# A sliding-window attention and SwiGLU kernel: a staged prologue, and q, k and x transposed by DMA instead of on TensorE

## The chip, the cores and the metric

The kernel runs on one core of one Trainium2 chip. The metric is the device time of one execution in microseconds (us). The profile's span runs from the first to the last instruction and is about 1.7 us shorter than the time. Most figures inside an execution below are on the span's clock.

The text uses the profile's names: PE is TensorE, PEld its weight loads, DVE VectorE, ACT ScalarE, POOL GpSimd, SP SyncE; SPq is the time in which SP issues a DMA. L327 is line 327 of that kernel's file, and the same function can have another line number in another kernel.

## The reference

```python
# q, k, v: [8 batches, 8 heads, 576 positions, 64], float32
scores = (1 / 8) * q @ k.transpose(0, 1, 3, 2)
mask = (rel >= 0) & (rel < 64)                 # rel = query position - key position
attn = softmax(where(mask, scores, -1e9)) @ v
x = attn.transpose(0, 2, 1, 3).reshape(4608, 512)
g = x @ w_gate                                 # 512 x 1536
out = (g * sigmoid(g) * (x @ w_val)) @ w_out   # 1536 x 512, result float32
```

## The kernel before

The 4608 tokens are cut in 36 chunks of 128 (n) for the attention and in 9 groups of 512 (c) for the gate, value and output products. For a chunk, `T` transposes k and q, `Sx` makes the scores of four heads, `AV` multiplies with v and divides by the row sum into `xb`, and `X` transposes `xb` into `xT`. `F(c, f)` makes one 128-wide slice of gate and value for 512 tokens, `O(c, u)` the output of 128 tokens. All of it is bf16 with float32 sums. A helper records the operations in program order, and each engine executes its own in that order, waiting on semaphores. In the main loop, chunk n = 4c+u+4 runs ahead of the group that needs it:

```python
def T(self, n):                      # on TensorE: 8 transposes into one bank, 3 evacuations
    def pe(e):
        for w, src in ((0, kn), (1, qn)):
            for c in range(4):
                r = e.transpose(tb[:, w, c, :], src[:, 2 * c:2 * c + 2, :], ident[:, :])
        return r
    ...  # DVE copies k into kT, ACT and DVE one half each of q into qz (its other half is zero)

for c in range(1, NFC):
    for u in range(4):
        n = 4 * c + u + 4
        load(n + 4)
        self.F(c, 3 * u);     self.AV(n, 0); self.Sx(n + 1, 0)
        self.F(c, 3 * u + 1); self.AV(n, 1); self.Sx(n + 1, 1)
        self.O(c - 1, u);     self.X(n)       # cut: conditions for the ends, and c == 1
        self.F(c, 3 * u + 2); self.T(n + 2)   # k and q two chunks ahead
```

The softmax here doesn't subtract the row's maximum and nothing guards it: scores larger than these inputs give would overflow.

Of the kernel before, what the change touches and what calls it, by code (L numbers as in the profile page):

```python
# [149 lines left out]
class _Kernel:  # L150
    NQ = 4
    NV = 8
# [13 lines left out]
    def alloc(self):  # L166
# [9 lines left out]
        self.mask = sb("mask", 4 * 64)  # L176
        self.Wg = sb("Wg", NK * DFF)[:, :].rearrange("p (c f) -> p c f", c=NK)
# [3 lines left out]
        self.qn = [hd(t) for t in ring("qn", self.NQ, DM)]  # L181
        self.kn = [hd(t) for t in ring("kn", self.NQ, DM)]
# [3 lines left out]
        self.qza = sb("qz", self.NZ * 4 * 2 * 128)[:, :].rearrange("p (r c e t) -> p r c e t", r=self.NZ, c=4, e=2)  # L186
        self.qz = [self.qza[:, r] for r in range(self.NZ)]
        self.fq, self.fk = [t[:, :].rearrange("p (h j d) -> p h j d", h=H, j=4) for t in ring("f", 2, H * 256, F32)]
        self.cq, self.ck = [t[:, :].rearrange("p (j h d) -> p j h d", j=4, h=H) for t in ring("c", 2, H * 256)]
        self.nmask = sb("nmask", 4 * 64)  # L190
# [4 lines left out]
        self.xT = [t[:, :].rearrange("p (c t) -> p c t", c=NK) for t in ring("xT", self.NX, NK * 512)]  # L195
        self.sig = ring("sig", self.NS, 512)
        self.uu = ring("uu", self.NS, 512)
        self.hT = [t[:, :].rearrange("p (f t) -> p f t", f=NF) for t in ring("hT", self.NH, NF * 512)]
# [22 lines left out]

    def init(self):
        g = self.g
        ident, mask = self.ident, self.mask
        g.op("dve", lambda e: e.memset(self.wz[:, :], 0.0), writes=["wz"])
        g.op("dve", lambda e: e.memset(ident[:, :], 0.0), writes=["ident"])  # L226
        g.op("dve", lambda e: e.memset(self.nmask[:, :], 0.0), writes=["nmask"])
        g.op("dve", lambda e: e.memset(mask[:, :], 1.0), writes=["mask"])
        g.op("dve", lambda e: e.memset(self.wup[:, :], 0.0), writes=["wup"])
        g.op("act", lambda e: e.activation(self.wup[:, :], self.wup[:, :], ACTF.Exp), writes=["wup"])  # L230
        zz = self.qza
        g.op("dve", lambda e: e.memset(zz[64:128, :, :, 0, :], 0.0), writes=[("qz", i, p, 0) for i in range(self.NZ) for p in range(4)])
        g.op("dve", lambda e: e.memset(zz[0:64, :, :, 1, :], 0.0), writes=[("qz", i, p, 1) for i in range(self.NZ) for p in range(4)])
        g.op("dve", lambda e: e.memset(self.kT[:, :, 0:64], 0.0), writes=[("kT", -1, p) for p in range(4)])
        g.op("dve", lambda e: e.memset(self.vb[0][0:64, :, 0:66], 0.0), writes=[("vb", 0, 0)])
        self.init_va(0)

    def init_pt(self):
        g = self.g
        for i in range(self.NP):  # L240
            p = self.pt[i]
            g.op("dve", lambda e, p=p: e.memset(p[:, :, 64:128], 0.0), writes=[("pt", i, 0), ("pt", i, 1)])

    def init_va(self, i0):
        g = self.g
        for i in range(i0, i0 + 4):
            va = self.va[i]
            g.op("dve", lambda e, va=va: e.memset(va[:, :, 64:80], 1.0), writes=[("va", i)])

    def init_pool_a(self):  # L250
        ident = self.ident
        self.g.op("pool", lambda e: e.affine_select(
            out=ident[:, :], in_=ident[:, :], compare_op=ALU.not_equal, fill=1.0, base=0,
            pattern=[[-1, 128]], channel_multiplier=1), writes=["ident"])
# [11 lines left out]
    def load_qk(self, n):  # L266
        i = n % self.NQ
        for dst, src, nm in ((self.qn[i], self.q, "qn"), (self.kn[i], self.k, "kn")):
            parts = list(self.segs(128 * n, 128))
            for j, (r, b, s, L) in enumerate(parts):  # L270
                d = dst[r:r + L]
                a = src[b, :, s:s + L, :].rearrange("h p d -> p h d")
                ks = [(nm, i, j)] if len(parts) > 1 else [(nm, i, 0), (nm, i, 1)]
                self.g.op("pool", lambda e, d=d, a=a: e.dma_start(d, a), writes=ks, dma=True)  # L274

    def first_loads(self):
        for half in range(2):
            hs = slice(4 * half, 4 * half + 4)
            for eng, dst, src, nm in (("sp", self.fk, self.k, "fk"), ("act", self.fq, self.q, "fq")):
                d = dst[:, hs].rearrange("p h j d -> p h (j d)")  # L280
                a = src[0, hs, 0:512, :].rearrange("h (p j) d -> p h (j d)", j=4)
                self.g.op(eng, lambda e, d=d, a=a: e.dma_start(d, a), writes=[(nm, half)], dma=True)

    def first_cast(self, which, half):
        hs = slice(4 * half, 4 * half + 4)
        dst, src, eng = (self.ck, self.fk, "dve") if which == "k" else (self.cq, self.fq, "act")
        d = dst[:, :, hs].rearrange("p j h d -> p h j d")
        rk, wk = [("f" + which, half)], [("c" + which, half)]
        if eng == "dve":
            self.g.op("dve", lambda e: e.tensor_copy(d, src[:, hs]), reads=rk, writes=wk)  # L290
        else:
            self.g.op("act", lambda e: e.activation(d, src[:, hs], ACTF.Copy), reads=rk, writes=wk)

    def first_T(self, which, half):
        g = self.g
        bank, bk = self.bank("a")
        tb = bank[:, :].bitcast(BF).rearrange("p (c j t) -> p c j t", c=2, j=4)
        src = self.ck if which == "k" else self.cq

        def pe(e):  # L300
            for c in range(2):
                pr = 2 * half + c
                for j in range(4):
                    r = e.transpose(tb[:, c, j, :], src[:, j, 2 * pr:2 * pr + 2, :], self.ident[:, :])
            return r

        g.op("pe", pe, reads=["ident", ("c" + which, half)], writes=[bk])
        prs = slice(2 * half, 2 * half + 2)
        if which == "k":
            kd = self.kT[:, prs, 64:576].rearrange("p c (t j) -> p c t j", j=4)  # L310
            ks = tb.rearrange("p c j t -> p c t j")
            kk = [("kT", n, p) for n in range(4) for p in (2 * half, 2 * half + 1)]
            g.op("dve", lambda e: e.tensor_copy(kd, ks), reads=[bk], writes=kk)
            return
        for e_, eng in ((0, "act"), (1, "dve")):
            ps = slice(64 * e_, 64 * e_ + 64)
            zk = [("qz", n, p, e_) for n in range(4) for p in (2 * half, 2 * half + 1)]

            def ev(e, ps=ps, e_=e_, eng=eng):
                for c in range(2):  # L320
                    d = self.qza[ps, :, 2 * half + c, e_, :].rearrange("p r (t j) -> p r t j", j=4)
                    a = tb[ps, c].rearrange("p j (r t) -> p r t j", r=4)
                    r = e.activation(d, a, ACTF.Copy) if eng == "act" else e.tensor_copy(d, a)
                return r

            g.op(eng, ev, reads=[bk], writes=zk)

    def warm(self, count):
        bank, bk = self.ps[7], ("ps", 7)

        def pe(e):
            for _ in range(count):
                r = e.matmul(bank[:, :], self.wz[:, 0:128], self.wz[:, :], start=True, stop=True)
            return r

        self.g.op("pe", pe, reads=["wz"], writes=[bk])

    def load_v(self, n):
        g = self.g
        i = n % self.NV  # L340
        va = self.va[i]
        parts = list(self.segs(128 * n, 128))
        for j, (r, b, s, L) in enumerate(parts):
            d = va[r:r + L, :, 0:64]
            a = self.v[b, :, s:s + L, :].rearrange("h p d -> p h d")
            ks = [("va", i, j)] if len(parts) > 1 else [("va", i, 0), ("va", i, 1)]
            g.op("pool", lambda e, d=d, a=a: e.dma_start(d, a), writes=ks, dma=True)  # L347
        vb = self.vb[i]
        lo = [("va", i, 0), ("va", i)]
        hi = [("va", i, 0 if len(parts) == 1 else 1), ("va", i)]  # L350
# [16 lines left out]

    def T(self, n):
        g = self.g
        iq, iz = n % self.NQ, n % self.NZ  # L370
        qn, kn, qz = self.qn[iq], self.kn[iq], self.qz[iz]
        bank, bk = self.bank("a")
        tb = bank[:, :].bitcast(BF).rearrange("p (w c t) -> p w c t", w=2, c=4)
        ident = self.ident

        def pe(e):
            for w, src in ((0, kn), (1, qn)):
                for c in range(4):
                    r = e.transpose(tb[:, w, c, :], src[:, 2 * c:2 * c + 2, :], ident[:, :])  # L379
# [339 lines left out]
```

## Time and profile before

The median time is 373.5 us (2 runs, 373.46 to 373.55). The span is best cut in three. The marks are the starts, in the trace, of ScalarE's first tanh of group c=2 and of group c=8 (each follows the first gate product of its group by about 1 us):

| part | before, us | what is in it |
|---|---|---|
| early, to c=2 | 99.0 | loads of weights, attention of chunks 0 to 11, c=0, c=1 |
| steady, c=2 to c=7 | 229.5 | 24 periods, median 9.64 |
| tail, c=8 | 43.3 | no attention left |

The chain that ended last in the kernel before, between 182 and 193 us: start, duration, what.

```profile
182.18 0.22 PE ps L460 x4
182.41 1.73 PE ps L485 x8
184.13 0.45 PE ps L379 x8
184.58 1.73 PE ps L485 x8
186.31 0.03 PE ps L438
...
186.55 0.28 PE ps L408 x4
186.83 1.73 PE ps L485 x8
...
188.84 0.40 PE ps L408 x4
189.24 0.05 issue
189.29 2.54 PE ps L508 x11
```

One period is all PE: three gate/value groups (L485), one output group (L508), the k/q transposes (L379, 0.45 us), the x transposes (L460, 0.22 us), scores (L408) and AV (L438 and L439). Time is saved there by taking work off TensorE, or by making its pieces shorter.

### The profile page before, as it was taken

Reading aid. Unit: us, or ns where it says so; the run is one execution under the profiler, and the core shown is the slowest. Engines: PE = TensorE matmul, PEld = TensorE weight load, DVE = VectorE, ACT = ScalarE, POOL = GpSimd, SP = SyncE. Lnnn points to the kernel's source line nnn. Section 1 sums busy time; section 2 is a strip of 40 time slices with the busy share of each in tenths; the row PEclk is TensorE's granted clock in tenths of the full one; section 3 lists DMA queues with packets and bytes.
Section 4 is the critical chain, followed back from the end, with each engine's and each line's share of the span. In section 5 each row is a group of like instructions: output and inputs, shape, how many; then the busy total and the mean of one; then the engine's idle time right before and its main releaser. Section 6 shows DMA issues by size and latency. Waiting matters only on the chain.

```text
span 371.8 us, 6649 instructions
## 1 busy us (share of the span) xinstructions
PE 353.7 (95%) x2604; PEld 193.6 (52%) x2649; DVE 254.5 (68%) x550; ACT 151.9 (41%) x260; POOL 108.6 (29%) x139
## 2 busy tenths in 40 slices
PE   6779989999899999999999999999999999999997
PEld 2644555555455555555555555555555555444444
DVE  5758876688867777777777777777777777645530
ACT  2743625445444344343344444434434444233321
POOL 8995435343222222322222222422220000000000
PEclk9899999999999999999999999999999999999999
DMA  8999999979947777788878877788881000001002
GB/s 237 201 203 175 206 171 216 173 53 86 86 69 86 88 84 87 82 89 88 91 81 92 86 83 79 74 85 90 88 90 37 30 29 30 28 30 56 28 30 113
DMA packets 126302, 35.61 MB, mean 96 GB/s; under 512 B 108288, under 2 KB 121792, under 8 KB 126272
## 3 DMA queue, kind: packets, MB, share of 16 engines
q0 software_dynamic: 113152, 17.83, 64.8%
q1 hardware_dynamic: 11920, 16.18, 13.5%
q10 hardware_dynamic: 1200, 1.18, 1.0%
q8 instruction: 21, 0.34, 0.4%
q14 instruction: 9, 0.07, 0.1%
HBM read 37.75 MB, written 9.44 MB: 127 GB/s over the span
## 4 chain that ended last, share of the span: by engine, by line
PE 79%; DVE 12%; DMA 4%; ACT 2%; issue 2%; SPq 1%; POOLq 0%
PE ps L485 41%; PE ps L508 24%; PE ps L408 5%; DVE uu L493 4%; DVE hT L495 3%; PE ps L379 3%; DMA va<-in_v_dram 2%; PE ps L460 2%; PE ps L438 2%; PE ps L439 2%; DVE xb L448 2%; DMA vb<-va 2%; ACT sig L491 1%; DVE pt L426 1%; ACT qz L385 1%
## 5 line engine op out<-in xcount | busy, mean ns | idle before, releaser
L493 DVE SCALAR_TENSOR_TENSOR uu<-sig,ps 128x512 bf16<-128x512 bf16 x108 | 74.1, 686 | 62.5 <-ACT sig L491 62.4
L485 PE MATMUL ps<-xT,Wv 128*128 128x512 bf16 x430 | 110.8, 379 | 0.1
L485 PE MATMUL ps<-xT,Wg 128*128 128x512 bf16 x408 | 105.7, 379 | 3.8 <-DVE xT L467 1.7
L508 PE MATMUL ps<-Wo,hT 128*128 128x512 bf16 x401 | 93.2, 379 | 2.0 <-DVE rc L445 1.0
L491 ACT ACTIVATE sig<-ps 128x512 bf16<-128x512 f32 x108 | 64.0, 592 | 44.3 <-PE ps L485 44.3
L274 POOL DMA_DIRECT2D qn<-in_q_dram x36 | 30.6, 853 | 163.0 <-PE ps L379 160.7
L495 DVE SCALAR_TENSOR_TENSOR hT<-uu,ps 128x512 bf16<-128x512 bf16 x108 | 74.2, 687 | 3.7
L485 PEld LDWEIGHTS ps<-xT,Wv 128*128 128x128 bf16 x432 | 42.3, 98 | 51.0
L508 PEld LDWEIGHTS ps<-Wo,hT 128*128 128x128 bf16 x420 | 39.8, 98 | 43.9 <-DVE hT L495 1.0
L420 ACT ACTIVATE pt<-ps 128x512 bf16<-128x512 f32 x72 | 42.8, 597 | 33.5 <-PE ps L408 30.9
L485 PEld LDWEIGHTS ps<-xT,Wg 128*128 128x128 bf16 x432 | 38.3, 98 | 32.6 <-DVE xT L467 2.0
L513 ACT ACTIVATE ost<-ps 128x512 f32<-128x512 f32 x35 | 20.9, 597 | 70.5 <-PE ps L508 70.5
L385 ACT ACTIVATE qz<-ps 64x512 bf16<-64x512 bf16 x32 | 18.9, 591 | 57.8 <-DVE kT L384 57.8
L347 POOL DMA_DIRECT2D va<-in_v_dram x40 | 34.7, 876 | 1.3 <-DVE ident L226 0.8
L408 PE MATMUL ps<-qz,kT 128*128 128x128 bf16 x288 | 30.4, 224 | 2.0 <-ACT qz L385 0.4
L448 DVE TENSOR_TENSOR xb<-ps,rc 128x256 bf16<-128x256 f32 x72 | 30.6, 425 | 2.5
L274 POOL DMA_DIRECT2D kn<-in_k_dram x36 | 30.7, 859 | 0.8 <-DMA Wv<-in_moe_w_val_dram 0.8
L467 DVE COPY xT<-ps 128x512 bf16<-128x512 bf16 x32 | 13.6, 424 | 24.0 <-PE ps L460 24.0
L438 PE MATMUL ps<-vb,pt 128*128 128x65 bf16 x288 | 26.9, 193 | 1.0 <-issue 0.4
L426 DVE TENSOR_TENSOR pt<-pt,mask 128x512 bf16<-128x512 bf16 x64 | 26.6, 416 | 1.5 <-ACT pt L420 1.4
L438 PEld LDWEIGHTS ps<-vb,pt 128*128 128x128 bf16 x288 | 22.5, 98 | 8.7 <-issue 1.1
L439 PE MATMUL ps<-va,pt 128*128 128x65 bf16 x288 | 27.0, 193 | 0.0
(54 smaller groups left out, 208.2 us busy)
## 6 DMA issues: line engine op xcount, KB each, us to landing
out_dram<-ost SPq DMA_DIRECT2D x35, 256.0 KB, 2.0
vb<-va SPq DMA_DIRECT2D x71, 80.0 KB, 2.1
va<-in_v_dram POOLq DMA_DIRECT2D x32, 128.0 KB, 4.5
qn<-in_q_dram POOLq DMA_DIRECT2D x28, 128.0 KB, 3.5
kn<-in_k_dram POOLq DMA_DIRECT2D x28, 128.0 KB, 4.4
Wo<-in_moe_w_out_dram POOLq DMA_DIRECT2D x2, 768.0 KB, 17.8
Wg<-in_moe_w_gate_dram POOLq DMA_DIRECT2D x5, 256.0 KB, 10.9
Wv<-in_moe_w_val_dram POOLq DMA_DIRECT2D x5, 256.0 KB, 11.5
```

The costliest lines, as they stand in the source:

```text
L274: self.g.op("pool", lambda e, d=d, a=a: e.dma_start(d, a), writes=ks, dma=True)
L347: g.op("pool", lambda e, d=d, a=a: e.dma_start(d, a), writes=ks, dma=True)
L408: r = e.matmul(sv[:, w, c], self.kT[:, pr, k0:k0 + 128], qz[:, pr, :, 64 * w:64 * w + 64], start=not bias, stop=True)
L420: g.op("act", lambda e: e.activation(po, si, ACTF.Exp, scale=SCALE), reads=[bk], writes=[pk])
L438: e.matmul(av[:, j, :], pt[:, h, 0:128], vb[:, h, 0:65], start=True, stop=False)
L439: r = e.matmul(av[:, j, :], pt[:, h, 64:192], va[:, h, 0:65], start=False, stop=True)
L448: g.op("dve", lambda e: e.tensor_tensor(xo, av[:, :, 0:64], rb, ALU.mult), reads=[bk, ("rc", ir)], writes=[("xb", ix, half)])
L485: r = e.matmul(bank[:, :], W[:, kk, f * 128:f * 128 + 128], xT[:, kk, :], start=(kk == 0), stop=(kk == NK - 1))
L491: g.op("act", lambda e: e.activation(sig[:, :], G[:, :], ACTF.Tanh, scale=0.5), reads=[gk], writes=[("sig", i)])
L493: g.op("dve", lambda e: e.scalar_tensor_tensor(uu[:, :], sig[:, :], 1.0, G[:, :], ALU.add, ALU.mult), reads=[("sig", i), gk], writes=[("uu ...
L495: g.op("dve", lambda e: e.scalar_tensor_tensor(hT[:, f, :], uu[:, :], 0.5, V[:, :], ALU.mult, ALU.mult), reads=[("uu", i), vk], writes=[(" ...
L508: r = e.matmul(OB[:, :], hT[:, f, 128 * u:128 * u + 128], self.Wo[:, f, :], start=(f == 0), stop=(f == NF - 1))
```

## The change

Its intent is to take every transpose off TensorE from chunk 4 on, and to start the products sooner.

1. Chunks 0 to 3 run in two stages of 256 tokens, with scores on PE tiles of 64 rows, and the first two gate/value groups are cut in halves around the second stage.
2. From chunk 4 on, k, q and x are transposed by DMAs on the sync queue. q is loaded into a buffer with zeros between the heads, so that its transpose has the zero halves that the scores need: 128x1024 instead of 128x512.
3. The later weights are loaded between chunks 4 to 7, and the padding of q is zeroed before that, by VectorE.
4. The order of c=0 and c=1 is new, with half-width groups in c=1.

```diff
     def T(self, n):
-        (8 PE transposes and 3 evacuations)
+        g.op("sp", lambda e: e.dma_start_transpose(kd, kn), reads=[("kn", iq, j) for j in range(2)],
+             writes=[("kT", n)], dma=True)
+        g.op("sp", lambda e: e.dma_start_transpose(qd, qn), reads=[("qn", iq, j) for j in range(4)],
+             writes=[("qz", iz)], dma=True)
+    def X(self, n):
+        self.g.op("sp", lambda e: e.dma_start_transpose(xo, xb), reads=[("xb", ix, 0), ("xb", ix, 1)],
+                  writes=[("xT", it, u)], dma=True)
     def A(self, n):
             self.AV(n, 0)
             self.AV(n, 1)
+            self.X(n)
+    def prep(self, n):
+            self.T(n)
+            self.shift_v(n)
... (prologue, loads, c=0 and c=1 cut)
-        for c in range(1, NFC):
+        for c in range(2, NFC):
             for u in range(4):
                 n = 4 * c + u + 4
-                load(n + 4)
+                self.load(n + 3)
                 self.F(c, 3 * u)
-                    (AV(n, 0), Sx(n + 1, 0))
+                self.A(n)
+                self.prep(n + 1)
                 self.F(c, 3 * u + 1)
-                    (AV(n, 1), Sx(n + 1, 1))
+                if n + 1 < NCH:
+                    self.Sx(n + 1, 0)
                 self.O(c - 1, u)
-                    (X(n))
+                if n + 1 < NCH:
+                    self.Sx(n + 1, 1)
                 self.F(c, 3 * u + 2)
-                    (T(n + 2))
```

## The prediction

> **What bounds it now.** TensorE. The page gives PE 95% of the 371.8 us span, and the chain of waits is 79% PE, 12% DVE. In steady state (chain from 170 to 220 us) one 128-token period is 9.63 us, all PE: three gate/value groups of 1.73, one output group 2.59, the q/k transposes 0.45, the x transposes 0.22, AV 0.50, scores 0.68 with small gaps. Before that, the first gate/value matmul starts at 24.8 us, held by the v loads and v shifts (the chain shows 9.0 and 5.6 us of DMA), and from 34 to 51 us the chain runs on VectorE.
>
> **What the change removes.** For 32 chunks the q/k and x transposes: 32 x 0.67 = 21 us of PE time, all critical in steady state. VectorE loses 1.27 us per chunk (0.42 + 0.43 + 0.42) and ScalarE 0.59. This should largely remove the VectorE-bound stretch at 34 to 51 us. The staged prologue should start the gate/value matmuls some 6 us sooner. With nothing new in the way, I estimate 343 to 353 us.
>
> **What it adds, and where it lands.** On the sync queue, per chunk: transposes of x(n), k(n+1), q(n+1), beside two v shifts and an output store. The order is the problem. That queue issues in program order, and x(n) comes first: it waits for xb(n), the last VectorE work of AV(n). So k(n+1) and q(n+1) can't be issued earlier, though their inputs have long been loaded. On PE, scores of n+1 follow AV(n) after one gate/value group only, 1.73 us.
>
> Timed from the end of the group before AV(n): scores could start at 0.50 + 1.73 = 2.23 us. xb(n) is done at about 2.65 us: final uu and hT 0.7 each, two reciprocal and multiply pairs of 0.6. Then three issues and a landing. Ordinary copies on this queue take 0.34 to 0.60 us to issue and land 2.0 to 2.1 us after issue; no transposing DMA is in this trace. The Trainium skill ("VectorE: DVE Perf Modes", The three transpose paths) gives 1309 ns for one 128x128 through the DMA crossbar, against 390 on TensorE; here q alone is eight such blocks, half of them zero padding. I estimate 0.5 + 0.5 us for the issues ahead of q and 2.8 us for q: scores start at 6.4 us, a PE stall near 4.2 us in each of 23 periods. The period becomes about 13 us instead of 8.96, and VectorE and DMA have slack in it.
>
> **Sum.** c=0 and c=1: no VectorE stretch and an earlier start, but stalls at the scores of chunks 8, 11 and 12 and at the xT halves, so c=2 starts at about 95 us (before: 96). Then 24 x 13.1 = 314, and the tail without attention 44: about 450 us. Even with 2.3 us of stall per chunk it is near 400.
>
> **Prediction:** 450 us, 80% range 398 to 520. Faster by over 2%: 0.06; within 2%: 0.04; slower by over 2%: 0.90.
>
> **What would show it.** Right: PE waits of 3 to 6 us before the score matmuls, released by the DMA into kT or qz, once per chunk from c=2 to c=7; the sync queue waiting for xb; PE busy below 85%; a period of 12 to 15 us up to the last attention chunk, then 7.8 us. The first gate/value matmul before 20 us. Wrong: the scores not waiting, and a period near 9 us.
>
> **What would make it wrong.** Transposes that land in well under 2 us, which would leave about 390. Long issue times (over 1 us each), DMA contention with the loads (4.2 us to landing now) or a lower granted clock after the stalls would bring 500 or more. Late weights, now split by chunk loads, could add to the first 100 us.

## More of the kernel before

The page of the kernel before: the span; then PE's busy time; then, in 40 equal slices of the span, PE's busy tenths and the clock granted to TensorE in tenths.

```profile
span 371.8 us, 6649 instructions
...
PE 353.7 (95%) x2604; PEld 193.6 (52%) x2649; DVE 254.5 (68%) x550; ACT 151.9 (41%) x260; POOL 108.6 (29%) x139
...
PE   6779989999899999999999999999999999999997
...
PEclk9899999999999999999999999999999999999999
```

## The result, and the profile after

The changed kernel takes 595.3 us (2 runs, 594.8 to 595.8) against 373.5: the ratio is 1.594, with a 95% interval of 1.589 to 1.598. Ratios in this text are the mean time of one kernel's fast runs over that of the other's of the same rounds, so they are not quite the ratio of the medians quoted. The result is correct. The forecast of slower was right; its 450 us, and its range up to 520, were not.

| part | before | forecast | after |
|---|---|---|---|
| early, to c=2 | 99.0 | about 98 (95, where it counts 96 for the kernel before; 99.0 on this mark) | 151.0 |
| steady, 24 periods | 229.5 | 314 | 399.8 |
| tail | 43.3 | 44 | 43.3 |
| median period | 9.64 | 13.1 | 17.06 |

The same lines of the page, for the changed kernel:

```profile
span 594.1 us, 6153 instructions
...
PE 399.7 (67%) x2337; PEld 193.8 (33%) x2337; DVE 222.6 (37%) x472; ACT 132.4 (22%) x232; POOL 129.6 (22%) x173
...
PE   6676367744666777666667766666677666669998
...
PEclk9598787878788877778888777788877777888999
```

PE has fewer instructions and more busy time, and its clock stays at seven or eight tenths in the mean of a slice until the attention is over (inside a period it is half or full, see below). One period of the chain of the changed kernel shows both reasons:

```profile
355.42 0.70 DVE uu L521
...
356.14 0.69 DVE hT L524
...
357.51 0.42 DVE xb L387
357.93 0.61 DVE uu L521
358.54 0.62 SPq L394
359.16 0.04 issue
359.20 1.26 SPq L327
...
360.56 3.06 DMA qz<-qn
...
363.67 0.61 PE ps L351 x4
364.28 4.70 PE ps L561 x12
368.98 0.22 PE ps L351 x4
369.20 2.60 PE ps L503 x12
```

VectorE ends xb of chunk n at 357.93. Then SyncE issues x (L394; its instruction starts at 357.96 and takes 1.20 us), then k of chunk n+1 (L327, 1.26 us), then q, which lands 3.06 us after its issue begins. Only then can the scores (L351) start. TensorE has had nothing for 5.84 us. And the output group that follows (L561, 12 matmuls) takes 4.70 us instead of 2.59: its weight loads are 0.43 us apart, twice the 0.216 that a matmul of 512 columns takes elsewhere. The clock records of the trace give 0.50 from 361.60 to 368.43 (6.83 us) and 1.00 for the 10.24 us before and after; TensorE has work for 4.76 of those 6.83 us. All 23 periods of the steady part that hold attention show the same two lengths, in sum 17.07 us, and the median period is 17.06.

The waits of the changed kernel's engines, then of its sync queue (engine, line, what it waited for: us in total, times, longest), three and one of many:

```profile
PE ps L351 <- DMA qz<-qn: 156.3, 29, 7.6
POOL qn L287 <- DVE qn L234: 22.5, 1, 22.5
PE ps L503 <- DMA xT<-xb: 16.8, 2, 9.4
```

```profile
SPq L394 <- DVE uu L521: 141.7, 25, 9.7
```

The first line is the wait described above. The last is x at the head of the sync queue, waiting for VectorE (the profile names the VectorE instruction that runs beside the end of xb) while k and q, long loaded, stand behind it. The two others belong to the early part: the load of q of chunk 4 stands 22.5 us in the GpSimd queue behind the zeroing of its padding, with the weights and loads of later chunks behind it; and twice the products of c=1 wait for x.

The DMA issues of the changed kernel (what, queue, count, KB each for plain copies, median us from the start of the issue to landing):

```profile
out_dram<-ost SPq DMA_DIRECT2D x35, 256.0 KB, 2.0
...
kT<-kn SPq DMA_TRANSPOSE x32, 2.5
...
qz<-qn SPq DMA_TRANSPOSE x32, 3.1
xT<-xb SPq DMA_TRANSPOSE x32, 2.3
```

### The profile page after: what moved, and what is told of

Read it like the earlier page. It is cut to its first block, busy times and chain, and to the rows that moved or that the text cites. A ratio compares the mean times of both kernels' runs of the same rounds, so it can differ in the third digit from the quotient of the medians.

```text
span 594.1 us, 6153 instructions
## 1 busy us (share of the span) xinstructions
PE 399.7 (67%) x2337; PEld 193.8 (33%) x2337; DVE 222.6 (37%) x472; ACT 132.4 (22%) x232; POOL 129.6 (22%) x173
## 4 chain that ended last, share of the span: by engine, by line
PE 48%; DMA 20%; DVE 15%; SPq 10%; ACT 3%; issue 2%; POOL 1%; POOLq 0%
PE ps L561 23%; PE ps L503 19%; DMA qz<-qn 16%; SPq L327 6%; DVE uu L521 6%; DVE xb L387 5%; PE ps L351 4%; DVE hT L524 4%; SPq L394 3%; ACT sig L513 3%; DMA va<-in_v_dram 2%; DVE rc L381 1%; DMA Wg<-in_moe_w_gate_dram 1%; DMA vb<-va 1%; POOL qn L287 1%
## 5 line engine op out<-in xcount | busy, mean ns | idle before, releaser
L561 PE MATMUL ps<-Wo,hT 128*128 128x512 bf16 x420 | 144.2, 517 | 0.0
L351 PE MATMUL ps<-qz,kT 128*128 128x128 bf16 x256 | 30.4, 262 | 157.1 <-DMA qz<-qn 156.3
L503 PE MATMUL ps<-xT,Wg 128*128 128x512 bf16 (+1 forms) x464 | 119.0, 382 | 24.0 <-DMA xT<-xb 16.8
L503 PE MATMUL ps<-xT,Wv 128*128 128x512 bf16 (+1 forms) x464 | 117.9, 379 | 0.0
L521 DVE SCALAR_TENSOR_TENSOR uu<-sig,ps 128x512 bf16<-128x512 bf16 (+1 forms) x114 | 74.9, 657 | 70.8 <-ACT sig L513 70.6
L513 ACT ACTIVATE sig<-ps 128x512 bf16<-128x512 f32 (+1 forms) x114 | 65.6, 575 | 124.9 <-PE ps L503 124.9
L561 PEld LDWEIGHTS ps<-Wo,hT 128*128 128x128 bf16 x420 | 54.0, 131 | 79.5 <-issue 62.9
L351 PEld LDWEIGHTS ps<-qz,kT 128*128 128x128 bf16 x256 | 20.6, 115 | 175.9 <-DMA qz<-qn 168.5
L524 DVE SCALAR_TENSOR_TENSOR hT<-uu,ps 128x512 bf16<-128x512 bf16 (+1 forms) x114 | 75.1, 659 | 5.2 <-PE ps L503 1.2
L287 POOL DMA_DIRECT2D qn<-in_q_dram x72 | 53.3, 765 | 49.4 <-DMA qz<-qn 24.0
L296 POOL DMA_DIRECT2D va<-in_v_dram x40 | 36.2, 909 | 6.5 <-DMA Wo<-in_moe_w_out_dram 4.1
L375 PEld LDWEIGHTS ps<-va,pt 128*128 128x128 bf16 x288 | 19.7, 99 | 3.4
```

What stands on the lines that cost most here:

```text
L287: self.g.op("pool", lambda e, d=d, a=a: e.dma_start(d, a), writes=ks, dma=True)
L296: self.g.op("pool", lambda e, d=d, a=a: e.dma_start(d, a), writes=ks, dma=True)
L351: r = e.matmul(sv[:, w, c], self.kT[:, pr, k0:k0 + 128], qz[:, pr, :, 64 * w:64 * w + 64], start=True, stop=True)
L375: r = e.matmul(av[:, j, :], pt[:, h, 64:192], va[:, h, 0:65], start=False, stop=True)
L503: r = e.matmul(bank[:, lo:hi], W[:, kk, f * 128:f * 128 + 128], xT[:, kk, lo:hi], start=(kk == 0), stop=(kk == NK - 1))
L513: self.g.op("act", lambda e: e.activation(sig[:, lo:hi], G[:, lo:hi], ACTF.Tanh, scale=0.5), reads=[gk], writes=[("sig", i)])
```

## The experiments

The theory: the loss in the steady part comes from the order on the sync queue (k and q behind x, and only 1.73 us of work between AV and the next scores), plus a second cost that TensorE's clock falls in the gap. The rival: transposing DMAs are too slow, or crowd out the loads, wherever they stand. For the early part: is it the transposes, the zeroing in the queue, or the staged prologue? Runs e1 to e4 are single runs, of state unknown, beside 373.14 us for the kernel before on the same chip; their effects are far over the noise. e4's is the smallest, 7 us, and is read from its early part: where that part is unchanged from the changed kernel, or nearly (e1, e2, e3), c=2 starts at 151.4 to 152.0 against 151.0, so this mark is good to about 1 us. The others have three rounds. All nine gave correct results.

A warning on marks: some expectations below count c=2 of the changed kernel from 131 us. What the trace has there is the tenth of the twelve groups of c=1 (its tanh at 131.7); c=2 starts at 151.0. Bounds for c=2 that were set from 131 are therefore too early for it.

### e1_ahead: k and q one chunk further ahead

```diff
+        self.prep(13)
         for c in range(2, NFC):
 ...
-                self.prep(n + 1)
+                self.prep(n + 2)
```

> One change to the changed kernel: from c=2 on, the k and q transposes are queued for chunk n+2 instead of n+1, at the same place of the sync queue, so a whole period ahead of the scores that read them. Theory (order): the 5.8 us PE wait before the scores comes from k and q standing behind x(n) on the in-order queue with only 1.73 us of PE work to cover it; it vanishes, the output group goes back from 4.70 to 2.6 us because TensorE no longer idles, the period falls from 17.0 to 9.0 to 9.6 us and the time to 400 to 415 us. Rival (the transposing DMAs are too slow or crowd out the loads): moving them does not help; the period stays above 13 us and the time above 500 us.

Measured: 406.0 us. The median period is 8.70 us, and the steady part 209.0 instead of 399.8. A period of its chain:

```profile
196.90 1.67 PE ps L503 x7
198.57 0.22 PE ps L351 x4
198.79 2.59 PE ps L561 x12
201.38 0.22 PE ps L351 x4
201.60 2.60 PE ps L503 x12
```

No DMA is in it, and the output group is back at 2.59. The same number of transposes with the same bytes now costs TensorE nothing, so the rival falls for the steady part. The period is also 0.94 us shorter than before the change, more than the 0.67 us of transposes. The rest is the loop's new order: e5 below runs it with the transposes on TensorE and has 9.37 us, so the order gives 9.64 - 9.37 = 0.27 and the transposes 9.37 - 8.70 = 0.67. Most of the 0.27 is in the score halves, 0.22 us each here and 0.28 and 0.40 in the kernel before. The early part stays at 152.0.

### e2_xpe: x back on TensorE, k and q untouched

```diff
-                self.A(n)
+                if n < NCH:
+                    self.AV(n, 0)
+                    self.AV(n, 1)
                 self.prep(n + 1)
 ...
                     self.Sx(n + 1, 1)
+                if n < NCH:
+                    self.Xpe(n, "dve")
```

> One change to the changed kernel: from c=2 on, x is transposed on TensorE again (after the second score half), k and q stay on the DMA for chunk n+1, at their old place. Theory (order): nothing that waits for xb stands ahead of k and q on the sync queue any more, so the stall vanishes although k and q are transposed no earlier in the program; period 9.2 to 10 us, time 405 to 425 us. Rival (k and q transposes themselves are too slow, 1.3 us to issue and 3.1 us to land): a stall of several us stays, time above 480 us.

Measured: 412.1 us, median period 8.93. Here k and q of chunk n+1 stand at their old place in the program, only x no longer stands before them. So it is x at the head of the queue (its wait for xb, and the 1.20 us of its issue) that made them late, not the distance in the program alone. The 0.23 us over e1 are what the x transposes cost TensorE.

### e3_fill: keep TensorE busy in the gap

```diff
+                    self.fill(20)      # 20 matmuls of 128x512 zeros into the output bank, overwritten after
                     self.Sx(n + 1, 0)
```

> One change to the changed kernel: 20 matmuls on zeros (512 columns, 4.3 us at the full clock) fill TensorE just before the first score half from c=2 on, inside the 5.8 us wait. They compute nothing that is used. Theory (the clock is a cost of its own, caused by the idle gap): the wait for q stays, but the output group after it runs at the full clock, 2.6 instead of 4.7 us, the granted clock goes from 0.79 to above 0.93 and the period from 17.0 to about 14.9; time 540 to 550 us. Rival (the low clock has another cause, or the fill comes on top of the wait): output group stays at 4.7 us, time 590 us or more.

Measured: 544.9 us, median period 14.76, granted clock 1.00 between 152 and 500 us (it was 0.80 in the steady part of the changed kernel). From its chain:

```profile
334.80 3.06 DMA qz<-qn
...
337.90 0.40 PE ps L351 x4
338.30 2.59 PE ps L571 x12
```

q lands just as late, but the output group takes 2.59 us again. The clock is a cost of its own, 17.06 - 14.76 = 2.30 us per period, and idling causes it: what fills the gap computes nothing, and the clock stays up. The wait proper is what is left between here and e1: 14.76 - 8.70 = 6.06 us.

### e4_early: zero two of the padded buffers at the start

```diff
         self.init_va(0, 4)
+        for i in range(4, self.NQ):
+            self.zero(self.qn[i][:, :, 1:3, :], [("qn", i, j) for j in range(4)])
 ...
-        for i in range(self.NQ):          # in init_late, after the first two groups
+        for i in range(4):
```

> One change to the changed kernel: the zeroing of the padding of q buffers 4 and 5 is done at the start on VectorE instead of after the first two gate/value groups. Theory: in the changed kernel the GpSimd queue stands 22.5 us (15.6 to 38.1 us) behind that zeroing before it may load q of chunk 4, and everything behind it in the queue (weights 8 to 12, output weights, chunks 5 to 9) is late; with the early zeroing the 4.5 us wait for the weights and the 9 us waits on xT and q between 60 and 100 us shrink, c=2 starts at 110 to 120 instead of 131 us, and the time is 572 to 586 us. Rival (the early loss is from the transposes crossing the load burst, whenever it comes): gain under 5 us.

Measured: 588.0 us, c=2 at 142.9 instead of 151.0, both on the mark of the table. The time lies outside the expected 572 to 586 us, and the gain of 8 us is less than was expected (on the mark at 131.7 it is 122.8, against 110 to 120). The 4.5 us wait for the gate weights is gone from the list of waits, but the waits for q before c=2 are 21.3 us in sum (21.2 in the changed kernel) and those for x 13.1 (16.8). So the zeroing in the queue explains 8 us of the early loss, and most of it must lie elsewhere.

### e5_pe: the changed kernel without any transposing DMA

`T` and `X` of chunks 4 to 35 go back to TensorE as in the kernel before, with q unpadded; the prologue, the order of loads and the half-width groups stay. The places of `T` and `X` in c=0 and c=1 had to be chosen anew, so this is not purely the change.

```diff
-                self.A(n)
-                self.prep(n + 1)
+                self.AV(n, 0); self.AV(n, 1)
+                self.prep(n + 2)                # T on TensorE
 ...
                     self.Sx(n + 1, 1)
+                if n < NCH:
+                    self.Xpe(n, "dve")
```

> The changed kernel with no transposing DMA at all: q, k and x of chunks 4 to 35 go back to TensorE (q loaded without padding, k and q transposed two chunks ahead, x after the next group), while the two-stage prologue with 64-row scores, the load order and the half-width groups of c=1 stay. It measures the prologue and the order alone. Theory: nearly all of the loss came with the transposing DMAs and their place in the queue; with them gone c=2 starts at 95 to 108 us instead of 131, the period is 9.4 to 9.7 us, and the time 372 to 388 us. Rival (the staged prologue and the reordered weights cost most of the 35 us lost before c=2): c=2 starts after 115 us, time above 395 us.

Measured: 386.5 us, ratio 1.036 (1.032 to 1.039). The time is in the expected range, but c=2 starts at 118.7 us, past the 115 that stood for the rival, and the period of 9.37 us makes up part of it. But the bound was set from 131; on that earlier mark e5 has 106.2, inside the expected 95 to 108. So the bound decides nothing, and the comparison on one mark has to. Of the 52.0 us lost early (151.0 - 99.0), 32.3 go away with the transposing DMAs and their padding (these include the 8.1 us of e4, as the padding is gone too), and 19.7 do not. The theory, that nearly all of the loss came with the transposing DMAs, was too generous to the rest of the change.

### e6_late: as e5, with transposing DMAs from chunk 12 on

```diff
-    (T and X on TensorE for every chunk)
+    def T(self, n):
+        (self.Tpe if n < 12 else self.Tdma)(n)
```

> As e5_pe, but from chunk 12 on k, q and x are transposed by DMA, two chunks ahead for k and q. Theory: the transposing DMAs are worth their 0.7 to 0.9 us of TensorE per period when nothing waits for them and the burst of weights is over: period 8.7 to 8.8 us as in e1_ahead, so 14 to 22 us less than e5_pe, time 352 to 370 us. Rival (they do harm wherever they run): not faster than e5_pe.

Measured: 379.4 us, ratio 1.016 (1.014 to 1.018), the same within 2% but slower clear of the noise. It is 7 us faster than e5, not 14 to 22. The median period is 8.70, but four periods took 9.1 to 9.8, and the early part is 3.7 us longer than in e5. The direction holds, the size was missed, and a kernel with the new prologue is still slower than the kernel before.

### e7_mix: the kernel before, with transposing DMAs from chunk 12 on

Up to chunk 11 it is the kernel before. From c=2 on:

```diff
                 load(n + 4)
                 self.F(c, 3 * u)
-                (AV and Sx halves)
+                self.A(n)
+                self.Xdma(n)
+                self.T(n + 2)                # by DMA, then the v shifts
                 self.F(c, 3 * u + 1)
+                self.Sx(n + 1, 0)
                 self.O(c - 1, u)
-                self.X(n)
+                self.Sx(n + 1, 1)
                 self.F(c, 3 * u + 2)
-                self.T(n + 2)
```

> The kernel before, unchanged up to chunk 11 (its prologue, its order of loads, TensorE transposes), and from chunk 12 on k, q and x transposed by DMA, k and q two chunks ahead, x straight after its AV. Theory: c=2 starts at about 96 us as before, then 24 periods of 8.7 to 8.8 us instead of 9.63, time 350 to 356 us, faster than the kernel before by 5 to 6 percent. If the staged prologue is a gain in itself, e6_late is the faster of the two; if it is a loss, this one.

Measured: 355.9 us, ratio 0.954 (0.952 to 0.956): faster than the kernel before. Most periods take 8.70 us, but four take 9.5 to 10.2 and one 9.0. A piece of its chain before such a period:

```profile
127.03 0.62 SPq L405
...
128.08 1.21 SPq L394
...
129.40 6.51 DMA qz<-f
...
135.95 0.40 PE ps L455 x4
```

q takes 6.51 us to land here, and one period of lead is just not enough.

### e8_prologue: the kernel before, with the staged prologue alone

```diff
-        for half in range(2): ...            # k and q of 512 tokens, in two halves of the heads
-        for n in range(4): self.Sx(n, 0, True) ...
+        self.first_cast("k", 0) ... self.first_S(0); self.first_S(1)
+        for n in range(2): self.AV(n, 0, True); self.AV(n, 1, True); self.Xpe(n, "dve")
+        self.F2(0, (0, 1), mid)              # mid: scores and AV of chunks 2 and 3
 ...
-        for f in range(6):
+        for f in range(2, 6):
             self.F(0, f)
```

> The kernel before with the staged prologue alone: chunks 0 to 3 in two 256-token stages, scores on 64-row tiles, the first two gate/value groups in halves around the second stage; everything from the third group on, all loads and all transposes as before. Theory: the stages put more small evacuations and waits in series than they take away and leave TensorE at the lower clock; the third group starts at 34 us instead of 28 as in the changed kernel, and VectorE, which bounds the stretch after it, starts its 1.4 us per group later, so c=2 starts 4 to 9 us later and the time is 377 to 383 us. Rival (the prologue is worth what it was meant to be, and the lost early time is all from loads, padding and order): 366 to 373 us.

Measured: 380.6 us, ratio 1.020 (1.018 to 1.021): slower clear of the noise, though whether by 2% is unclear. The first gate product starts earlier, at 22.1 us instead of 24.8, but the third gate/value group starts 7.1 us later than before (its tanh at 36.2 instead of 29.1), c=2 starts at 106.0 instead of 99.0, and from there on nothing differs. The stretches 12 to 25 us of the kernel before and of this one (busy time and count of each engine, granted clock, DMA), in this order:

```profile
12.00:25.00 13.00, 9.37 (x145) 8.35 (x147) 8.20 (x24) 7.85 (x14) 13.00 (x19) 0.87 1.49 213
```

```profile
12.00:25.00 13.00, 6.72 (x63) 5.12 (x63) 4.29 (x12) 2.48 (x4) 13.00 (x18) 0.61 1.57 208
```

PE (first number) does less there, VectorE and ScalarE (third and fourth) about half or less, and the granted clock is 0.61 instead of 0.87. The last of the shifted v copies lands at 21.3 us here and at 20.4 before, so late v data explain 1 us at most; the kernel before fills the wait with the scores of all four chunks, the staged one has only two chunks to work on, and then waits for xb before each of four x transposes (3.6 us in all; 1.0 us before).

### e9_lead: e7 with one more period of lead

```diff
+        load(16)
+        self.T(14)
         for c in range(2, NFC):
 ...
-                load(n + 4)
+                load(n + 5)
 ...
-                self.T(n + 2)
+                self.T(n + 3)
```

> e7_mix with one more period of lead from c=2 on: loads of chunk n+5 and k and q transposes of chunk n+3 in period n. In e7_mix five of 24 periods took 9.5 to 10.2 us instead of 8.70, with the scores waiting for q, while the DMA engines were busy 99% of the time. Theory (late landing, not lack of throughput): with the lead the waits vanish, all periods take 8.7 us and the time is 350 to 353 us. Rival (the DMA engines are full at 8.7 us per chunk): the backlog only moves, some periods still take over 9.3 us, time 354 to 357 us.

Measured: 351.1 us, ratio 0.941 (0.939 to 0.943). All periods take 8.70 us, but for the last, 8.3; the steady part is 208.4 us. It is the fastest kernel here, 5.9% under the kernel before. One period of its chain, and its transposing DMAs:

```profile
203.22 1.67 PE ps L532 x7
204.89 0.22 PE ps L455 x4
205.12 2.59 PE ps L555 x12
207.71 0.22 PE ps L455 x4
207.93 2.60 PE ps L532 x12
```

```profile
kT<-kn SPq DMA_TRANSPOSE x24, 4.2
qz<-f SPq DMA_TRANSPOSE x24, 5.3
xT<-xb SPq DMA_TRANSPOSE x24, 3.2
```

The transposes still land late, 5.3 us for q in the median, and the page's row of DMA busy tenths stands at 9 from 105 to 262 us, nearly as in e7. But TensorE no longer waits for them (the GpSimd queue does, before it loads q into a buffer again). A row of nines there did not mean that the transfers were the limit.

## Why the prediction was wrong

What held, step by step:

- TensorE as the bound, and the work taken off it. The forecast put 0.67 us per period; 9.64 - 8.70 = 0.94 was to be had (e1, e9), of which 0.67 are the transposes as forecast and 0.27 the loop's new order (e5), which it did not count.
- The mechanism. x stands ahead of k and q in an in-order queue and waits for xb; e1 and e2 each take this away in another way, and both remove the stall.
- The time of xb. The forecast had 2.65 us after the end of the group before AV; in the period shown the last value matmul ends near 355.45 and xb at 357.93, so 2.5 us.

What failed, in the forecast's own words:

1. "0.5 + 0.5 us for the issues ahead of q and 2.8 us for q: ... a PE stall near 4.2 us". The estimate carried over the issue times of plain copies, 0.34 to 0.60 us. A transposing DMA holds the queue for 1.20 us (x) and 1.26 us (k). q's landing, 3.06 us, was nearly right. From xb to the scores it put 3.8 us; in the period shown it took 5.74. The stall measured 6.06 us (e3 less e1; 5.84 in that period).
2. "The period becomes about 13 us". The sum had no term for the clock, which was named only among the risks. It is 2.30 us per period (e3). The Trainium skill ("TensorE: Matmul & The Clock Gate", Part 1, What's actually happening) says that TensorE falls to half its clock after an idle window of about 3.4 us and needs a busy one to come back. This case agrees: a gap of 5.84 us, then 4.70 us for 2.59 us of work; the clock falls to 0.50 at 361.60, 3.8 us after TensorE's work ends, and is back 4.8 us after work begins again. The forecast put the stall over that limit and still costed the work after it at full speed. Together, -0.94 + 6.06 + 2.30 = 7.42 us per period, the measured 17.06 - 9.64. That the sum closes proves nothing, since its terms are differences between these same periods; a check from inside one period is the wait of 5.84 us, and the slow scores and output group, 0.61 + 4.70 instead of 0.40 + 2.59 us, which is 2.32 more.
3. "an earlier start, ... so c=2 starts at about 95 us" and "The first gate/value matmul before 20 us". It started at 21.7 us, 3.1 earlier than before and not 6, and c=2 came 52.0 us later than before, not slightly earlier. The staged prologue, put down as a gain of 6 us, loses 7.0 (e8). The zeroing that blocks the GpSimd queue costs 8.1 (e4) and was not seen in the diff at all. Another 24.2 us (32.3 - 8.1) go with the transposing DMAs of chunks 4 to 11 (e5 against the changed kernel): there the scores wait as later on, and q takes over 8 us to land twice in the chain. The remaining 12.7 us (19.7 - 7.0), by subtraction and not by a run of their own, belong to the order of c=0 and c=1; since e5 has its own order there, how much of it is the change's stays open. Open too is how much of the 24.2 us is late landing in the burst of loads and how much the place in the queue; no run here separates them. The trace shows both at work: the first six q transposes take 5.4 to 10.5 us to land, the 26 from 109 us on about 3.1, and in the burst one k holds the queue for 2.27 us and one q for 3.92.

Of the 141 us between the 453 of the forecast's sum and the span of 594, about 86 lie in the steady part (points 1 and 2) and 53 in the early part (point 3); the rest is the 3 us between the forecast's mark of c=2 and the table's.

## What to carry to other kernels

When work moves from a compute engine to a queue that issues in order, look at what stands ahead of it there: a transfer whose inputs are long ready is as late as the slowest wait before it, and the repair can be one number in the program (n+1 to n+2, worth 189 us here). Cost a stall on TensorE with the clock that it takes away from the work after it, and cost a new kind of DMA with its own issue time, measured in a small run, not with that of a copy. When several changes come together, run each alone: the transposing DMAs and the new order of the loop were worth 6% here, with lead and after the load burst (of 22 us, about 24 x 0.67 = 16 are the transposes', by e5; the kernel before with the new order alone was not run), while the prologue that came with them cost 2% by itself.

## What the Trainium skill lacked or had wrong

- "Advanced Engine Details and Errata", X-Bar Transpose (TRN2), says that transposing DMAs are as fast as regular ones. Here they held the sync queue for 1.19 to 1.27 us (medians) against 0.34 to 0.60 for plain copies. In landing the difference is not clear: 2.3 to 3.1 us against 2.0 for a 256 KB store and 3.1 for the 80 KB copies of v that follow them on the queue. No page that we read gives, for this chip by name, the issue time of a transposing DMA, or says that it hardly depends on size: k (128x512) took 1.27 us and q (128x1024) 1.25 in the median.
- "VectorE: DVE Perf Modes", The three transpose paths, gives 1309 ns for one 128x128 block by DMA. It does not say how this grows with blocks: x, four blocks, landed in 2.3 us and q, eight blocks, in 3.1. From these two we estimate 0.2 us per block and a fixed part of 1.5.
- "DMA: Bandwidth & Descriptors" has no figure for a transpose beside heavy loads. The same q transpose had a median of 3.1 us in the changed kernel, 5.3 in e9_lead with faster periods, and took 8.3 to 10.5 us for five of the first six in the load burst of the changed kernel's early part.
- "TensorE: Matmul & The Clock Gate" has the rule about gaps right. Here one gap cost 2.30 us: after 5.84 us of idling the next 12 matmuls of 512 columns took 4.70 instead of 2.59 us. What it lacks is that a loop can settle on the clock's steps: half for 6.83 us and full for 10.24 in each of 23 periods, 17.07 in sum, and a median period of 17.06. Whether these steps hold the period there, no run tests.
